# Limits for VectorE's exp tiles by segment, a new searched plan, and tie-breaking offsets in a self-scheduled Conformer block

One core of one Trainium2 chip. The metric is the device time in microseconds (us) of that core, as the median of repeated executions; the kernel before takes 931.73 us (three runs, 931.69 to 931.85). "The trace" is one profiled execution, with the start and length of every instruction on TensorE (PE; its weight loads are PEld), VectorE (DVE), ScalarE (ACT) and GpSimd (POOL).

## The reference

One Conformer block in bfloat16 on two sequences of 4000 tokens, width 144, 4 heads of 36. The softmax of the attention is the large part.

```python
B, T, D, K, H = 2, 4000, 144, 5, 4
x = x + 0.5 * (silu(layernorm(x) @ w_ff1a) @ w_ff1b)          # FF1
q, k, v = split(layernorm(x) @ w_qkv)                         # 4 heads of 36
p = softmax(einsum('bhqd,bhkd->bhqk', q, k) * 36 ** -0.5)     # 2 x 4 x 4000 x 4000
x = x + (p @ v) @ w_o
a, b = split(layernorm(x) @ w_pw1)
c = depthwise_conv5(a * sigmoid(b), dw)
x = x + silu(c) @ w_pw2
x = x + 0.5 * (silu(layernorm(x) @ w_ff2a) @ w_ff2b)          # FF2
return layernorm(x)
```

## The kernel before

The kernel works in 16 chunks of 500 tokens. A tile of the softmax is a block of keys times 500 queries for 4 heads; most tiles are 128x1000 in PSUM. Instructions are not written down in their final order. The kernel is a program of coroutines ("threads") with a list scheduler that runs while the kernel is built: it keeps an estimated clock for every engine, picks the thread that can go next, and records its instruction. The finished list is then replayed with semaphores. So the order on each engine is fixed when the chip runs it, and waits are as long as reality makes them.

```python
# Rec.op: what the planner thinks of an instruction
start = ready = self.free[eng]
for d, raw in o.deps:
    if d.eng != eng or d.q is not None or (raw and eng != "pe"):
        ready = max(ready, d.done + self.SEM[eng])
# ...
self.free[eng] = o.t1 = start + cost          # cost is a number that the kernel gives
```

The exp of a tile is done by one ScalarE instruction, or by VectorE in seven (per half a linear step that writes the bits of a 16-bit float, then a correction over both halves). `due()` decides on VectorE, from limits that are partly tables by segments of 21 tiles (`now("...")`) and partly constants (FDVE, FEQ; PRELAG in `lag()`).

```python
def emit_exp(n, lo, hi):                                           # ScalarE's way
    # ...
    op("act", "activation", PT[:, pt, :, :], PSV[:, lo:hi + 1, 0:CH], ACT.Exp, bias=0.0, scale=ATT_SCALE, ...)

def due():                                                         # VectorE's turn?
    n = n_s[0]
    if n >= NIT or not DVE_EXP or live_dve[0] >= now("LIVE") or early[0] >= now("EARLY") or lag():
        return False
    ph, c, t = its[n]
    if len(kv_done) < CPB and (len(kv_done) < FDVE or len(eq) < FEQ):    # the front: keys still missing
        return False
    return (t <= phases[ph][2] - 7 and c in q_done and keys_in(c, t + 6)
            and R.free["dve"] < R.free["pe"] + now("DSLACK") and R.free["pe"] > last_dve[0] + now("DGAP"))
```

The front is the time in which the keys and values of the first sequence are still being made (8 chunks); the tail is what is left after the last attention matmul. A layer norm is divided differently in these than in the middle, where all of it but the statistics is GpSimd's:

```python
def ln(c, bs, e=False):                                            # cut
    # bn_stats on VectorE
    calm = mode["front"] or mode["tail"]
    op("dve" if calm else "pool", "tensor_scalar", RS[..., 1, 0:n], ST[..., 2], 1.0 / D, LN_EPS, ...)
    op("pool", "tensor_tensor", RS[..., 0, 0:n], RS[..., 1, 0:n], NHALF, op=ALU.pow, ...)
    if not calm:
        op("pool", "tensor_scalar", RS[..., 2, 0:n], ST[..., 1], -1.0, None, op0=ALU.mult, ..., cost=0.3)
        for j in range(n):
            op("pool", "tensor_scalar", XN[..., j, :], X[...], RS[..., 2, j:j + 1], RS[..., 0, j:j + 1], ..., cost=XN_COST)
    elif mode["tail"] and R.free["act"] + XSLACK < R.free["dve"]:  # on ScalarE
        ...
    else:                                                          # on VectorE
        ...

# the tail: earliest thread first
S.run(min((q for q in c if q[1].req.eng == eng), key=lambda q: q[0] + (q[1].rank >= 0) * TFIRST)[1])
```

The softmax here doesn't subtract the row's maximum and nothing guards it: scores larger than these inputs give would overflow.

## Time and profile before

| stage | from the trace of before |
|---|---|
| first exp starts | 20.30 us |
| keys of the 8th chunk are copied, the front ends | near 121 to 122 us |
| first exp on VectorE | 89.05 us |
| last exp ends | 896.08 us |
| tail, from there to the last instruction's end | 33.47 us |
| exp tiles | 855 wide on ScalarE, 137 on VectorE |

All instructions go through one helper, line 169, so they are told apart by tiles: PT the exps, PS a PSUM bank, TH tanh, XN a normalized block, RS and ST the statistics of a norm, HT the FF products, WA and WB the FF weights. A matmul that writes PS from IDENT alone is a filler: its result is not used, and the scheduler puts it on TensorE where its clocks foresee a wait.

A reading used throughout: ScalarE's *work* between the first and last exp is the sum of counts times paces (0.884 us from the start of one wide exp to the next, 0.467 for a 500-wide tanh, and so on). The *loss* is the length of that stretch less the work. Before, that is 875.8 - 843.9 = 31.9 us.

### The profile page before, as it was taken

The numbers are of one execution on the slowest core, as the hardware profiler recorded it, in microseconds if no ns is written. First come the engines' busy times: TensorE is split into PE (matmuls) and PEld (weight loads), VectorE is DVE, ScalarE is ACT, GpSimd is POOL, SyncE is SP. The second block draws the span as 40 slices with busy tenths as digits, with TensorE's granted clock in tenths as the row PEclk, the third lists the DMA queues.
The fourth block names the chain that finished last, engine by engine and source line by source line (L and its number), as shares of the span: only waits on it lengthen the run. The fifth ranks groups of instructions, "written<-read, shape, count | busy, mean of one in ns | idle before, by whom it ended". The sixth has DMA issues, their size and how long they took to land.

```text
span 929.6 us, 26576 instructions
## 1 busy us (share of the span) xinstructions
PE 886.9 (95%) x11413; PEld 405.4 (44%) x11413; DVE 849.9 (91%) x1880; ACT 895.0 (96%) x1142; POOL 306.1 (33%) x520
## 2 busy tenths in 40 slices
PE   8999999999999999999999999999999999999997
PEld 7444433434344344344443443443444343434456
DVE  8886799999989999998999999898999999997997
ACT  6899999999999999999999999999999999999985
POOL 4220140182115412351512452225415331441433
PEclk9999999999999999999999999999999999999999
DMA  4000000000000000000000000000000000000000
GB/s 124 22 2 1 2 2 1 1 2 1 2 2 2 2 2 2 2 2 1 9 1 1 14 2 8 2 1 14 2 8 3 7 2 9 8 1 8 8 2 26
DMA packets 7449, 7.30 MB, mean 8 GB/s; under 512 B 2381, under 2 KB 7332, under 8 KB 7332
## 3 DMA queue, kind: packets, MB, share of 16 engines
q1 hardware_dynamic: 5918, 5.00, 1.8%
q8 instruction: 89, 1.46, 0.6%
q10 hardware_dynamic: 1414, 0.62, 0.3%
q14 instruction: 28, 0.23, 0.1%
HBM read 3.31 MB, written 2.30 MB: 6 GB/s over the span
## 4 chain that ended last, share of the span: by engine, by line
ACT 47%; PE 36%; DVE 14%; issue 1%; POOL 1%; DMA 0%; POOLq 0%; DVEq 0%
ACT PT L169 41%; PE PS L169 36%; DVE PT L169 8%; ACT TH L169 5%; DVE ST L169 2%; DVE HT L169 1%; DVE X L169 1%; DVE QT L169 1%; DVE OTF L169 1%; POOL RS L169 0%; DMA X<-in_x_dram 0%; DVE DG L169 0%; POOL XN L169 0%; DVE XN L169 0%; DVE XT L169 0%
## 5 line engine op out<-in xcount | busy, mean ns | idle before, releaser
L169 ACT ACTIVATE PT<-PS 128x1000 bf16<-128x1000 f32 (+1 forms) x871 | 802.4, 1053 | 6.8 <-PE PS L169 5.2
L169 PE MATMUL PS<-QT,KT 64*64 64x500 bf16 x3968 | 413.9, 385 | 20.3 <-ACT PT L169 14.2
L169 PE MATMUL PS<-PT,VA 64*37 64x500 bf16 x3968 | 353.4, 374 | 4.9 <-DVE OTF L169 2.2
L169 PEld LDWEIGHTS PS<-QT,KT 64*64 64x64 bf16 x3968 | 122.4, 104 | 219.7 <-ACT PT L169 139.1
L169 POOL TENSOR_SCALAR RS<-ST 125x4 f32<-125x4 f32 x112 | 41.6, 371 | 467.2 <-DVE ST L169 462.5
L169 DVE TENSOR_SCALAR PT<-PS 128x500 uint16<-128x500 f32 x274 | 183.0, 669 | 12.8 <-PE PS L169 11.5
L169 DVE TENSOR_TENSOR PT<-PT 128x1000 uint16<-128x1000 uint16 (+1 forms) x274 | 184.0, 676 | 1.5
L169 DVE TENSOR_SCALAR PT<-PT 128x1000 uint16<-128x1000 uint16 (+1 forms) x411 | 163.8, 415 | 2.3
L169 PEld LDWEIGHTS PS<-PT,VA 64*37 64x37 bf16 x3968 | 114.1, 95 | 111.1 <-issue 31.9
L169 POOL TENSOR_SCALAR XN<-X,RS 125x144 bf16<-125x144 bf16 x224 | 149.9, 680 | 5.8
L169 POOL TENSOR_TENSOR RS<-RS,NHALF 125x4 f32<-125x4 f32 (+1 forms) x103 | 100.5, 980 | 112.5 <-DVE RS L169 107.8
L169 ACT ACTIVATE TH<-PS 128x500 bf16<-128x500 f32 (+2 forms) x198 | 104.3, 549 | 5.0 <-PE PS L169 4.3
L169 DVE SCALAR_TENSOR_TENSOR HT<-TH,PS 128x500 bf16<-128x500 bf16 (+1 forms) x135 | 80.8, 614 | 9.6 <-ACT TH L169 9.4
L169 PE MATMUL PS<-XT,WA 72*128 72x500 bf16 (+2 forms) x288 | 73.8, 355 | 2.9 <-DVE HT L169 1.6
L169 DVE SCALAR_TENSOR_TENSOR X<-PS,X 125x288 bf16<-125x288 f32 x128 | 57.0, 451 | 15.3 <-PE PS L169 13.6
L169 DVE BATCH_NORM_STATS2 ST<-X 125x6 f32<-125x288 bf16 x160 | 65.5, 446 | 1.2 <-DMA X<-in_x_dram 1.0
L169 PE MATMUL PS<-WB,HT 128*125 128x144 bf16 (+1 forms) x640 | 52.8, 230 | 0.5 <-DVE HT L169 0.5
L169 PEld LDWEIGHTS PS<-WB,HT 128*125 128x125 bf16 (+1 forms) x640 | 44.1, 136 | 14.0 <-issue 4.2
L169 PE MATMUL PS<-IDENT,XN 125*72 125x125 bf16 x512 | 42.2, 221 | 2.5 <-DVE HT L169 1.3
L169 DVE COPY XT<-PS 72x1000 bf16<-72x1000 bf16 (+1 forms) x66 | 39.9, 609 | 3.1 <-PE PS L169 2.6
L169 PEld LDWEIGHTS PS<-IDENT,XN 125*72 125x72 bf16 x512 | 31.5, 112 | 21.0 <-issue 10.6
L169 PE MATMUL PS<-U,DG 128*128 128x250 bf16 (+5 forms) x204 | 34.3, 265 | 0.6 <-DVE PT L169 0.4
(88 smaller groups left out, 579.6 us busy)
## 6 DMA issues: line engine op xcount, KB each, us to landing
X<-in_x_dram SPq DMA_DIRECT2D x16, 140.6 KB
out_dram<-XN SPq DMA_DIRECT2D x13, 140.6 KB
out_dram<-XN SPq DMA_DIRECT2D x4, 70.3 KB
WA<-in_w_ff1a_dram ACTq DMA_DIRECT2D x1, 144.0 KB
WB<-in_w_ff1b_dram ACTq DMA_DIRECT2D x1, 144.0 KB, 2.6
WA<-in_w_ff2a_dram SPq DMA_DIRECT2D x1, 144.0 KB
WB<-in_w_ff2b_dram SPq DMA_DIRECT2D x1, 144.0 KB
WQKV<-in_w_qkv_dram ACTq DMA_DIRECT2D x1, 121.5 KB
```

What stands on the lines that cost most here:

```text
L169: ins = getattr(eng, o.name)(*o.a, **o.k)
```

## The change

Its intent: constants that limit VectorE's exps become tables, so that the search can set them by segment; the offsets FJ (front) and TJ (tail), looked up by a thread's number, let the search break ties between threads; two switches of the tail get other thresholds; and the matmuls of a chunk's conv remainder wait by rule for the copy of the edge. All tables were searched anew.

```diff
+    TJ = (0.0, 0, 0.0, 0.0, -0.3, ... 48 offsets, 12 of them not zero)
+    FJ = [0.0, ... 0.25, ... -0.25, ... 64 offsets, 2 of them not zero]
+    FLEX = 0.3
 ... (the tables AHEAD to BGPICK: all new values but nothing else)
         "DSLACK": (
-            0.4, 0.4, 0.4, 0.2, 0.2, 1.5, ...
+            0.4, 0.4, 0.4, 2.5, 1.5, 1.5, ...
+        "FEQ": (2, 2, 2, 1, 2, ... 49 entries),
+        "FDVE": (5, 5, 5, 5, 5, ...),
+        "PRELAG": (0.7, ...),
+        "LAGD": (1, 0, 1, 1, ...),
-    FDVE = 5
-    FEQ = 2
-    PRELAG = 0.7
-        if mode["tail"] and R.free["act"] < R.free["dve"]:
+        if mode["tail"] and R.free["act"] + FLEX < R.free["dve"]:
-    XSLACK = 0.5
+    XSLACK = 1.2
-            bk = yield need("pe", banks, dur=0.17)
+            bk = yield need("pe", banks, dur=0.17, cond=lambda: c in left_done)
-        if ... or lag():
+        if ... or now("LAGD") and lag():
-        if len(kv_done) < CPB and (len(kv_done) < FDVE or len(eq) < FEQ):
+        if len(kv_done) < CPB and (len(kv_done) < now("FDVE") or len(eq) < now("FEQ")):
 ... (three other sort keys take FJ of the thread's number; the conv rule has one more wait, for the last chunk)
-    S.run(min((...), key=lambda q: q[0] + (q[1].rank >= 0) * TFIRST)[1])
+    S.run(min((...), key=lambda q: q[0] + (q[1].rank >= 0) * TFIRST + TJ[q[1].no % len(TJ)])[1])
```

## The prediction

> **What bounds the kernel now.** I read the busy table and the slices of the page first, then the busy times by stretch, the groups by form, the merged timeline of ScalarE and TensorE, and last the counts of instructions per engine in the changed kernel's order. The kernel carries its own list scheduler: the tables in the diff steer which thread goes next, and the arithmetic is the same. So the question is where an engine has room, and whether the new order uses it.
>
> ```profile
> PE 886.9 (95%) x11413; PEld 405.4 (44%) x11413; DVE 849.9 (91%) x1880; ACT 895.0 (96%) x1142; POOL 306.1 (33%) x520
> ...
> DVE  8886799999989999998999999898999999997997
> ACT  6899999999999999999999999999999999999985
> ...
> ACT 47%; PE 36%; DVE 14%; issue 1%; POOL 1%; DMA 0%; POOLq 0%; DVEq 0%
> ```
>
> Three engines are above 90% and the chain of waits hops between them, but ScalarE is the fullest: it is at 9 in all slices but the first two and the last two. The busy times by stretch (columns: stretch, its length, then busy us and count of PE, PEld, DVE, ACT and POOL, clock, DMA share, GB/s) split this by stage:
>
> ```profile
> 20.30:44.30 24.00, 21.78 (x229) 11.61 (x228) 20.98 (x60) 19.85 (x34) 5.58 (x8) 1.00 0.10 36
> 44.30:67.00 22.70, 22.11 (x296) 9.52 (x294) 18.93 (x59) 22.38 (x29) 5.53 (x8) 1.00 0.01 3
> 67.00:93.00 26.00, 25.38 (x309) 10.78 (x308) 17.45 (x37) 24.64 (x33) 1.36 (x2) 1.00 0.00 1
> 93.00:896.00 803.00, 772.33 (x10017) 333.81 (x10016) 751.23 (x1577) 796.80 (x982) 272.25 (x458) 1.00 0.01 4
> 896.00:929.50 33.50, 26.89 (x333) 23.31 (x329) 25.54 (x90) 20.25 (x46) 10.80 (x19) 0.98 0.06 18
> ```
>
> From 93 to 896 us ScalarE is busy 796.8 of 803.0, or 99.2%: that stretch shortens only if ScalarE is given less, or starts closer together. From 44.3 to 93 (the rest of the front, in which keys and values are still being made) ScalarE is also nearly full, 47.0 of 48.7, but VectorE has 48.7 - 18.93 - 17.45 = 12.3 us idle. The tail, after the last exp, is 33.5 us in which ScalarE has slack; there TensorE is the fullest.
>
> ```profile
> L169 ACT ACTIVATE PT<-PS 128x1000 bf16<-128x1000 f32 x855 | 794.4, 1061 | 5.6 <-PE PS L169 4.0
> L169 DVE TENSOR_SCALAR PT<-PS 128x500 uint16<-128x500 f32 x274 | 183.0, 669 | 12.8 <-PE PS L169 11.5
> L169 DVE TENSOR_TENSOR PT<-PT 128x1000 uint16<-128x1000 uint16 (+1 forms) x274 | 184.0, 676 | 1.5
> L169 DVE TENSOR_SCALAR PT<-PT 128x1000 uint16<-128x1000 uint16 (+1 forms) x411 | 163.8, 415 | 2.3
> ...
> 453.52 15.24 ACT PT L169 x17
> ```
>
> The first row is the exp of one tile of scores on ScalarE; the next three are the VectorE substitute, two plus two plus three instructions a tile, 137 tiles. The last line is from the chain in order of time: 17 exps take 15.24 us, 0.896 each. (The row's 1.061 us contains the overlap of neighbours. The median from one start to the next is 0.884.) So one tile moved away frees 0.884 us of ScalarE and costs VectorE (183.0 + 184.0 + 163.8) / 137 = 3.87 us.
>
> **What the Trainium skill says.** "ScalarE: Activation LUTs", section "What ACT_TABLE_LOAD costs", gives one element per cycle at 1.2 GHz, which is 833 ns for 1000 elements, plus a fixed part, with neighbours overlapping. The 0.884 measured here is 51 ns above that, so the pace of the exp is nearly all elements, and no order of instructions makes one cheaper. "VectorE: DVE Perf Modes", section "The perf-mode tier table (the rule you actually need)", puts a 16-bit tensor_scalar in SBUF at 4x, tensor_tensor at 2x, and anything from PSUM at 2x at most. The trace agrees in rank: 415 ns, 676 ns and 669 ns, the last for half as many elements. The substitute costs VectorE over four times what it saves ScalarE and pays only where VectorE idles. "Perfetto Trace Analysis", section "Optimization Strategy", says that kernels can have several regimes and may gain by interleaving them; the 12.3 us of idle VectorE beside a full ScalarE is such a place.
>
> **The change, part by part.**
>
> *Front limits.* FDVE, FEQ, PRELAG and the lag test become tables by segments of 21 tiles. The front ends after some 84 tiles, so only the first four or five entries of FDVE and FEQ can act there; FDVE stays 5 in them and FEQ falls from 2 to 1 in segment 3 (tiles 63 to 83), where the slack for VectorE (DSLACK 0.2 to 2.5) is also opened and the gap (DGAP 4.0 to 3.5) cut. The switch on lag can do nothing in the front, since the lag test answers no before all keys are in. The counts in the order show the effect. VectorE has 280 half-tile exps instead of 274, so 140 tiles instead of 137; ScalarE has 852 exps instead of 855. All three come early: ahead of the key copies of the eighth chunk VectorE has done 5 tiles instead of 2. In the trace the first VectorE exp starts at 89.0 us and those copies at 121. Saving on ScalarE: 3 x 0.884 = 2.65 us. Cost on VectorE: 3 x 3.87 = 11.6 us, which fits the 12.3 us idle, if barely. TensorE's 4 + 4 matmuls a tile stay.
>
> *Other ScalarE work between first and last exp.* By counts it rises by one tanh of 128x500 and one copy, some 0.47 us each: +0.9 us. Net there: -1.7 us.
>
> *Front ties (FJ).* Two non-zero entries swap a few threads. ScalarE does 7 exps in both before the pause in them that lies at 28.4 to 44.3 us. In the pause it now does 18 instead of 14 wide tanh and one more narrow one, counted from the first exp: 4 x 0.467 + 0.258 = 2.1 us more. The exps resume later by about that, but the same tanh are missing afterwards. I count zero. The eighth chunk's keys now come after 75 score tiles instead of 84, so the front is over earlier, which moves work and removes none.
>
> *Middle.* All search tables are redone. Start-to-start paces times counts (855 x 0.884, 137 x 0.467, 29 x 0.154, 27 x 0.258, 16 half exps and 11 copies at 0.47) make 844 us of the 875 between the first and last exp's start, so 31 us are lost, 4 to 5 of them in the pause and the rest in crumbs. New tables may regain or lose a few of these. I take -0.3 us.
>
> *Tail (TJ, FLEX, XSLACK).* After the last attention matmul the new order leaves two 500-wide tiles of FF2's first layer (four matmuls) and four pairs of pw2 matmuls less on TensorE: 4 x 0.215 + 8 x 0.065 = 1.4 us by the paces of the tail. It also does one chunk of FF2 in 500-wide matmuls that was done in 250-wide halves; at 0.215 us for one and 0.1075 for the other that is the same time. So an estimate of the real work left there goes from 22.9 to 21.5 us. One layer norm goes back to GpSimd ahead of the tail: ScalarE normalizes 2 rows' sets instead of 8. Instead, one FF2 chunk goes through tanh, which gives VectorE five more products, 4 x 0.666 + 0.407 = 3.1 us. VectorE has 8 us idle in the tail, so half of that may show as waits.
>
> ```profile
> 921.03 2.04 PE L169 MATMUL PS<-WB,HT 128*125 128x144 bf16 x30
> 922.92 0.81 DVE L169 SCALAR_TENSOR_TENSOR X<-PS,X 125x288 bf16<-125x288 f32 x2
> 925.24 1.21 DVE L169 TENSOR_SCALAR XN<-X,ST,RS 126x144 bf16<-126x144 bf16 x4 [0.24 <-POOL RS L169]
> ```
>
> Here 30 closing matmuls come in one batch, three residuals, statistics and norms queue behind them, and the span ends 6.5 us after TensorE does. The new order ends with 10, the other 20 lying earlier: some 0.5 us less. Tail in sum: -1.9 us, of which I give 0.4 back for the waits: -1.5.
>
> *Last conv waits for edges.* A condition that orders emission, for one chunk, behind a GpSimd copy that is long done: 0.
>
> Sum: -2.65 + 0.9 - 0.3 - 1.5 = **-3.6 us**, 931.7 to about **928.1 us**.
>
> **Rivals.** (a) *The moved tiles return as waits.* VectorE also serves the front's tanh products and copies; with 11.6 us more in 12.3 of idle time, TensorE waits for banks and ScalarE for TensorE. For: ScalarE and TensorE are both at 97% there, and the front's waits of VectorE are for TensorE and ScalarE, not free choice. Then the 2.65 us are lost: about 931. (b) *The search found more than counts show.* For: 31 us are lost between exps, and nearly every table is new. Against: the old tables came from the same sort of search, and the gaps that the trace shows on ScalarE from 93 to 896 are only 6 us. It would give 924 to 925. (c) *The tail gets longer.* Tanh makes two engines do what Silu did in one, and TensorE fillers stay at 37 against 36, so the new order expects as much idle time. Then the tail gives +1 in place of -1.5: 930 to 931. (d) *The real times differ from the scheduler's table*, and the order loses where an engine comes late: perhaps +2 us on any of these.
>
> **Range and chances.** The core is -3.6; (a), (c) and (d) pull up by 2 to 3, (b) down by 3 to 4. The range is 924.5 to 931.0. Two per cent is 18.6 us; no stage has that to give (the whole tail is 33.5, the moved tiles 2.65), and the work is the same, so a slowdown of that size is as far. Faster by over 2%: 0.01. Within 2%: 0.98. Slower: 0.01.
>
> **What would show it.** Right: 852 wide exps on ScalarE; VectorE's busy time up by some 10 us, with the 44 to 93 us stretch near 90% where it was 75%; the last exp's end 1.5 to 2.5 us earlier than 896.1; the stretch after it about 32 us. Wrong: the last exp ends no earlier, with more idle time before ScalarE's exps or TensorE's score matmuls in the front (rival a); the last exp ends over 4 us earlier (b); the tail is 34 us or more (c).

## The result

The changed kernel takes 928.27 us (four runs, 928.17 to 928.39), the kernel before 931.71 us in the same rounds (931.69 to 931.85): 3.44 us less. The ratio is 0.9963, with a 95% interval of 0.9946 to 0.998; within 2%. The prediction was 928.1 us, and its direction, class and range held.

The page of the changed kernel, its busy times, two rows of the slices and the shares of the chain that ended last:

```profile
PE 886.4 (96%) x11406; PEld 400.7 (43%) x11406; DVE 861.9 (93%) x1900; ACT 888.8 (96%) x1133; POOL 307.9 (33%) x524
...
DVE  7998999999999998798999999999999999998987
ACT  5799999999999999999999999999999999999985
...
ACT 48%; PE 34%; DVE 14%; POOL 2%; issue 1%; DMA 0%; POOLq 0%; DVEq 0%
```

VectorE took on 861.9 - 849.9 = 12.0 us of work (some 9.3 of it for the three tiles: so much it sheds when they are given back below); ScalarE gave up 6.2 us in the whole execution. GpSimd's share of the chain, 1% before, is now 2%: a small sign of what the experiments come to in the end. The same stretches as in the prediction, with the ends of the last two moved to this kernel's (columns: stretch, its length, busy us and count of PE, PEld, DVE, ACT, POOL, then clock, DMA share, GB/s):

```profile
20.30:44.30 24.00, 22.89 (x208) 11.64 (x200) 22.50 (x60) 20.09 (x36) 4.90 (x8) 1.00 0.11 40
44.30:67.00 22.70, 22.24 (x352) 11.23 (x352) 20.68 (x65) 19.95 (x27) 6.45 (x9) 1.00 0.01 3
67.00:93.00 26.00, 24.95 (x328) 10.46 (x324) 21.69 (x47) 25.89 (x34) 2.11 (x3) 1.00 0.01 1
93.00:893.50 800.50, 773.88 (x9998) 331.02 (x9989) 756.05 (x1587) 794.52 (x980) 270.70 (x455) 1.00 0.01 4
893.50:926.40 32.90, 25.34 (x304) 21.29 (x302) 25.50 (x85) 17.24 (x37) 13.31 (x25) 0.94 0.08 23
```

From 44.3 to 93 us VectorE is now busy 20.68 + 21.69 = 42.4 of 48.7 us, or 87%; it was 75%. The stretch from 93 us to the last exp is 2.5 us shorter (800.5 against 803.0), and ScalarE is as full in it as before, 794.52 of 800.50, or 99.3%. That is what a bound that was relieved of work looks like: the same fullness, a shorter stretch.

The groups by form give the counts, and the merged timeline gives the first VectorE exp of the changed kernel (columns of the timeline: start, length, engine, line, operation, tiles, shapes):

```profile
L169 ACT ACTIVATE PT<-PS 128x1000 bf16<-128x1000 f32 x852 | 792.3, 1063 | 6.3 <-PE PS L169 5.1
```

```profile
65.90 0.68 DVE L169 TENSOR_SCALAR PT<-PS 128x500 uint16<-128x500 f32 x1 [0.93 <-PE PS L169]
```

Three exps moved, and VectorE's first exp comes at 65.90 us instead of 89.05. ScalarE's timeline at the last exp, before and then after:

```profile
893.70 2.38 ACT L169 ACTIVATE PT<-PS 128x1000 bf16<-128x1000 f32 x3
```

```profile
891.81 1.66 ACT L169 ACTIVATE PT<-PS 128x1000 bf16<-128x1000 f32 x2
```

The last exp ends at 893.70 + 2.38 = 896.08 before, and at about 893.46 after: 2.6 us earlier. Where the rest lies:

| part | before | after | difference |
|---|---|---|---|
| first exp starts | 20.30 | 20.58 | +0.28 |
| ScalarE's work to the last exp | 843.9 | 842.2 | -1.7 |
| ScalarE's loss there | 31.9 | 30.7 | -1.2 |
| tail | 33.47 | 33.05 | -0.42 |
| span of the trace | 929.6 | 926.5 | -3.0 |

The two profiled executions differ by 0.4 us less than the medians. The first row is only scatter: in the other traces of these two plans the first exp starts anywhere from 20.42 to 20.74 us.

The gain was not built up evenly. By the start of a score tile's exp (tiles counted from 0), the new order is 4.0 us *behind* at tile 20 (61.1 against 57.1 us), 0.8 ahead at tile 63, 3.1 ahead at tile 84 (119.4 against 122.4), 2.3 behind at tile 400 and 3.0 ahead at tile 990. A lead in the middle of such a plan says little; only where the last exp ends counts.

And the tail, of which I had expected -1.5 us, gave -0.4. The closing matmuls and the last normalization, after:

```profile
919.10 0.84 PE L169 MATMUL PS<-WB,HT 128*125 128x144 bf16 x10
```

```profile
921.74 1.21 DVE L169 TENSOR_SCALAR XN<-X,ST,RS 125x144 bf16<-125x144 bf16 x4 [0.15 <-POOL RS L169]
```

The closing batch has 10 matmuls instead of 30, as foreseen, but the time from TensorE's end to the end is 6.58 us where it was 6.48: the smaller batch bought nothing. TensorE itself ends 26.47 us after the last exp instead of 26.99.

### The profile page after: what moved, and what is told of

It is laid out like the page before. It is cut to its first block, busy times and chain, and to the rows that moved or that the text cites. A ratio compares the mean times of both kernels' runs of the same rounds, so it can differ in the third digit from the quotient of the medians.

```text
span 926.5 us, 26578 instructions
## 1 busy us (share of the span) xinstructions
PE 886.4 (96%) x11406; PEld 400.7 (43%) x11406; DVE 861.9 (93%) x1900; ACT 888.8 (96%) x1133; POOL 307.9 (33%) x524
## 4 chain that ended last, share of the span: by engine, by line
ACT 48%; PE 34%; DVE 14%; POOL 2%; issue 1%; DMA 0%; POOLq 0%; DVEq 0%
ACT PT L169 43%; PE PS L169 34%; DVE PT L169 7%; ACT TH L169 5%; POOL RS L169 1%; DVE ST L169 1%; DVE HT L169 1%; DVE X L169 1%; DVE QT L169 1%; POOL XN L169 1%; DVE XT L169 0%; DMA X<-in_x_dram 0%; DVE OTF L169 0%; DVE SW L169 0%; DVE XN L169 0%
## 5 line engine op out<-in xcount | busy, mean ns | idle before, releaser
L169 POOL TENSOR_SCALAR RS<-ST 125x4 f32<-125x4 f32 x114 | 51.2, 449 | 461.6 <-DVE ST L169 456.1
L169 DVE TENSOR_TENSOR PT<-PT 128x1000 f16<-128x1000 f16 (+1 forms) x280 | 188.4, 677 | 1.5
L169 DVE TENSOR_SCALAR PT<-PT 128x1000 uint16<-128x1000 uint16 (+1 forms) x420 | 170.3, 418 | 2.8
L169 POOL TENSOR_SCALAR XN<-X,RS 125x144 bf16<-125x144 bf16 x228 | 142.4, 636 | 5.9
L169 POOL TENSOR_TENSOR RS<-RS,NHALF 125x4 f32<-125x4 f32 (+2 forms) x101 | 98.5, 980 | 96.5 <-DVE RS L169 91.7
L169 ACT ACTIVATE TH<-PS 128x500 bf16<-128x500 f32 (+2 forms) x203 | 108.2, 560 | 5.7 <-PE PS L169 5.2
L169 DVE SCALAR_TENSOR_TENSOR X<-PS,X 125x288 bf16<-125x288 f32 (+1 forms) x128 | 57.2, 451 | 7.5 <-PE PS L169 6.6
L169 PE MATMUL PS<-IDENT,XN 125*72 125x125 bf16 (+1 forms) x512 | 42.4, 221 | 3.7 <-DVE XN L169 1.7
L169 PEld LDWEIGHTS PS<-IDENT,XN 125*72 125x72 bf16 (+1 forms) x512 | 31.2, 112 | 23.9 <-issue 12.6
L169 PE MATMUL PS<-U,DG 128*128 128x375 bf16 (+5 forms) x204 | 34.0, 265 | 0.0
```

Of the source, the lines that this page charges most:

```text
L169: ins = getattr(eng, o.name)(*o.a, **o.k)
```

## The experiments

Twelve kernels ran, on several chips. Except for the last call the kernel before ran at medians of 931.71 to 931.88 us in all of them, so I compare medians with 928.27 us directly. (In the first eight, one of seven runs of the kernel before took 941 us at a granted clock of 0.986, which pulls its mean up and the ratios down; the medians are free of this. One run each of five of the kernels, and two of another, took some 0.9 to 1.6 us longer than the rest of the same kernel, at a granted clock of 0.996 instead of 0.998 or more; the traces read below are all of the quicker kind.) One part needed no run: with the conv rule alone undone, the order of instructions on every engine is identical. Its effect is 0 by construction.

### Parts of the change undone

**The tail's rules.**

```diff
-    TJ = (48 offsets)    FLEX = 0.3    XSLACK = 1.2
+    TJ = (0.0,)          FLEX = 0.0    XSLACK = 0.5
```

> The changed kernel with TJ all zero, FLEX 0 and XSLACK 0.5. The order up to the tail is the same, so the last exp must end at 893.5 us again. Theory (the counts made the tail shorter, and a held-up GpSimd ate most of it; the tie table is worth little by itself): about 929.3, that is +0.5 to +1.5 on 928.3. Rival (the tail rules are what the gain is made of): 931 or more. Second rival (they do nothing): within 0.3 of 928.3.

Measured: 928.68 us (928.67 to 930.15; ratio 0.9956). The last exp ends at 893.45, as in the changed kernel, and the tail is 33.41 us instead of 33.05. The tail's rules are worth 0.4 us, between what the theory and the second rival gave them. The trace says more: without these rules the removed work is gone from the tail all the same. Fillers left out, TensorE is busy after the last exp for 25.05 us in the kernel before, 23.46 in the changed one and 23.00 in this one. So the other tables removed that work, which by itself gave almost nothing (33.47 to 33.41 us; the hold-up of GpSimd that is told of below stands in this run too), and nearly all that the tail gained came with its rules.

**The old plan with the new thresholds.** All tables and limits of before, no offsets; only FLEX and XSLACK are new.

> The plan of the kernel before (all its tables, 137 tiles on VectorE, no offsets) with only the two new tail limits, FLEX 0.3 and XSLACK 1.2. Theory (the gain sits ahead of the last exp): no gain, 931 to 933, last exp ending at 896.1 as before. Rival (the tail limits alone give the gain): 928 to 929.

Measured: 931.84 us (931.80 to 931.84; ratio 0.9985), tail 33.63 us. The thresholds do nothing for the old plan; the 0.4 us belongs to offsets that were searched for this one.

**The limits.** FDVE, FEQ, PRELAG and LAGD as the constants of before, all other tables new.

```diff
+        "FEQ": (2,) * 49, "FDVE": (5,) * 49, "PRELAG": (0.7,) * 49, "LAGD": (1,) * 49,
```

> The changed kernel with FDVE, FEQ, PRELAG and the lag test back to their constants. Its order has 134 tiles on VectorE and 858 wide exps on ScalarE, six more than the changed kernel. Theory (each exp on ScalarE is worth its pace of 0.884 us): 6 x 0.884 = 5.3 us later last exp, at 898 to 900 us, and 933 to 936 in all. Rival (the gain is a matter of order and waits, not of counts): last exp within 2 us of 893.5, time under 931.

Measured: 952.58 us (952.47 to 952.75; ratio 1.0207). A miss by far: I had expected a few us. ScalarE does 858 wide exps instead of 852, its work is 6.5 us more, its loss 10.7 us more, and the tail 7.1 us longer (40.11); these three make the 24.3 us. Up to 101 us the two kernels are nearly the same. It is what comes later that went wrong: the other tables were tuned to the exact course that the limits gave, by the number of the tile, and on another course they fit nothing. So this run does *not* say that the limits are worth 24 us. It says that a searched plan can't be taken apart by its parameters; the following runs change instructions and leave the plan alone.

It does settle one thing that the prediction had otherwise. With the limits of before, VectorE's first five tiles are the same as in the changed kernel: 25, 40, 49, 54 and 69 of the score tiles, the first at 65.8 us. Before, it has two that early, tiles 47 and 55. So the early tiles don't come from the new limits, whose first changed entry for the front, in segment 3, acts from tile 63 on only. They come with the other tables. In both new orders the fifth chunk's keys, for which the limit FDVE asks, are there at 62.5 us instead of 69.5; whether that is the reason was not tested.

**The front's offsets.** `FJ = [0.0]`.

> The changed kernel with the two non-zero front offsets (FJ) set to zero. ScalarE and GpSimd keep their order exactly, TensorE and VectorE swap a few instructions. Theory (I counted zero for the front ties): 928.0 to 928.6. Rival (the ties are what makes the front faster): 929 or more.

Measured: 928.35 us (928.12 to 928.55; ratio 0.9948). Nothing, as predicted.

### Which engine binds, with the plan held fixed

In each of these, instructions of known size are added without telling the scheduler (cost 0 on its clocks), so that everything else keeps its place.

**ScalarE.**

```diff
+    if stats["exp"] in (150, 200, ..., 700):                       # 12 places
+        op("act", "activation", SCR[:, 0:500], WB1..., ACT.Copy, cost=0.0)
```

> The changed kernel with 12 more ScalarE copies of 128x500 into scratch, one every 50 exps, the order otherwise unchanged: 12 x about 0.48 = 5.8 us more work on ScalarE. Theory (ScalarE sets the length from 93 us on): +5 to +6 us, about 934. Rival (three engines bind in turn): +2 to +3.

Measured: 933.74 us (933.39 to 934.98; ratio 1.0007). The copies hold ScalarE for 12 x 0.51 = 6.1 us; the last exp ends 5.45 us later: 0.89 of what was added. This is what the theory expected.

**VectorE.** The same with 14 additions of 128x736 in scratch, 14 x 0.449 = 6.3 us.

> The changed kernel with 14 more VectorE additions of 128x736 into scratch, one every 43 exps, the order otherwise unchanged: 14 x about 0.45 = 6.3 us more work on VectorE. Theory (ScalarE binds, VectorE has some slack in the middle): +1 to +2.5 us. Rival (VectorE binds as well): +5 to +6.

Measured: 932.89 us (932.25 to 933.50; ratio 0.9997), the last exp 3.95 us later: 0.63. A miss; I had expected at most 2.5. (Of the four runs two took 932.3 and two, at a clock of 0.996, 933.5; the trace is of the first kind.) With the order fixed, VectorE's queue has little slack, though ScalarE is at 99%. The additions have two inputs in SBUF, so by the lock told of below they may hold up GpSimd as well. Its busy time rose by 3.2 us, but TensorE waited for its XN no longer than before (1.4 us); I take the figure as VectorE's.

**TensorE.** The scores of 42 tiles are computed twice, 42 x 0.215 = 9.0 us.

> The changed kernel with the score matmuls of 42 tiles done twice (same result), 42 x 0.215 = 9.0 us more work on TensorE, the order otherwise unchanged. Theory (TensorE is close behind ScalarE): +2 to +5 us. Rival (TensorE binds): +8 to +9.

Measured: 932.01 us (931.79 to 933.51; ratio 0.9989), the last exp 3.46 us later: 0.38, in the expected range.

**VectorE in the front of the kernel before.** 26 such additions between its 9th and 60th exp, 26 x 0.452 = 11.75 us: what the prediction counted for the three tiles, in the room that it called idle.

> The kernel before with 26 VectorE additions of 128x736 into scratch between its 9th and 60th exp (46 to 101 us), 26 x about 0.45 = 11.7 us, as much as three exp tiles cost there, with nothing taken from ScalarE. Theory (that room was free): 0 to +1.5 us, up to 933.2. Rival a (VectorE's work returns as waits): +3 or more.

Measured: 935.93 us (935.84 to 935.98; ratio 1.0028) against 931.88, with the last exp 4.57 us later: 0.39. A miss: I had expected the idle room to swallow nearly all of it, and it is rival a's number that came. Idle time that the page shows is not room for any work. What comes unplanned stands before something that another engine waits for: from 44 to 106 us TensorE's waits for VectorE's copies and products rise from 1.0 to 3.8 us, and those of ScalarE's exps for TensorE from 0.5 to 2.8 us.

### The three tiles themselves

**Front tiles back to ScalarE.** In the changed kernel the first three VectorE tiles are computed by ScalarE, as two 128x500 exps each. The scheduler's clock of VectorE still counts the seven instructions that are left out, so TensorE's and GpSimd's orders are exactly those of the changed kernel.

```diff
 def dve_tile(n):
+    started[0] += 1
+    if started[0] in (1, 2, 3):
+        yield from act_tile(n)       # op("act", "activation", PT[:, z, hh, :], PSV[:, bk, 0:CH], ACT.Exp, cost=0.0)
+        return
```

> The changed kernel with its first three VectorE exp tiles (66 us on) computed by ScalarE, six exps of 128x500 in their place, while the plan still counts VectorE's time for them: TensorE and GpSimd keep their order exactly, the rest of VectorE and ScalarE too. ScalarE gets 6 x 0.47 = 2.8 us more, VectorE loses 3 x 3.35 = 10 us. Theory (the three tiles moved are the saving of the front): +2 to +2.8 us, 930.3 to 931.1. Rival (VectorE's load costs about as much as ScalarE is spared, as added VectorE work cost 0.4 to 0.6 of its length): -1.5 to +0.5.

Measured: 931.30 us (930.99 to 932.16, five runs; ratio 0.9996): 3.0 us more, just over the expected range, and nearly the kernel before. Its busy times by stretch in the front:

```profile
44.30:67.00 22.70, 21.83 (x344) 10.86 (x340) 20.10 (x64) 19.96 (x28) 6.45 (x9) 1.00 0.01 3
67.00:93.00 26.00, 24.10 (x304) 9.96 (x304) 13.08 (x28) 25.89 (x37) 1.36 (x2) 1.00 0.00 1
```

VectorE is relieved of 8.6 us in the second stretch (13.08 against 21.69), yet the execution is longer. The last exp ends at 896.35, 2.9 us later. That is the length of six half exps (6 x 0.47 = 2.8). The rival that the moved tiles return as waits would have left the time where it was. The figure is the tiles' worth in this plan: the six exps come unplanned, and a search without the three tiles might have placed them more cheaply.

**Middle tiles back to ScalarE.** The same for the 50th, 75th and 100th VectorE tile.

```diff
-    BACK = (1, 2, 3)
+    BACK = (50, 75, 100)
```

> The same for the 50th, 75th and 100th VectorE tile, in the middle. ScalarE gets 2.8 us more, VectorE loses 10 us. Theory (ScalarE binds by nine tenths, what VectorE sheds is worth less when the plan holds its place): +1.5 to +2.8. Rival (VectorE binds as well): -2 to +0.5.

Measured: 930.92 us (930.90 to 932.50, five runs; ratio 0.9995): +2.65 us, as expected, with the last exp at 896.30. So a tile on VectorE is worth the same in the middle, where VectorE is busy for 94% (756.05 of 800.50), as in the front. So idle time beside it is not needed for a placed tile to pay. That the front's idle time is what let the search place three more there is likely, but not shown.

### The tail's missing microsecond

The trace of the changed kernel shows a strange thing just before the tail. First GpSimd's timeline, then VectorE's in the same time:

```profile
888.22 4.24 POOL L169 TENSOR_SCALAR RS<-ST 125x4 f32<-125x4 f32 x1
892.57 1.79 POOL L169 TENSOR_SCALAR XN<-X,RS 125x144 bf16<-125x144 bf16 x4
...
896.17 1.79 POOL L169 TENSOR_SCALAR XN<-X,RS 125x144 bf16<-125x144 bf16 x4
```

```profile
888.03 0.67 DVE L169 TENSOR_TENSOR PT<-PT 128x1000 f16<-128x1000 f16 x1
...
890.46 1.26 DVE L169 TENSOR_TENSOR PT<-PT 128x1000 uint16<-128x1000 uint16 x2
891.63 0.74 DVE L169 TENSOR_SCALAR PT<-PT 128x1000 uint16<-128x1000 uint16 x2
892.29 0.67 DVE L169 SCALAR_TENSOR_TENSOR HT<-TH,PS 128x500 bf16<-128x500 bf16 x1
```

The negation of four means, 125x4 numbers, takes 4.24 us; the median of its group is 0.233. It is let go when VectorE passes from its exp instructions in SBUF to a product that reads PSUM. The Trainium skill, "SBUF — State Buffer", section "Who interferes with whom", says that VectorE and GpSimd share one pair of ports as an exclusive lock: VectorE takes it in its two-port modes, and with two SBUF inputs against a GpSimd instruction that reads SBUF, and the other engine is blocked for the whole instruction. The trace agrees: nine VectorE instructions of just these two kinds run end to end from 888.03 to 892.37, and the hold ends with them. It is no single case. Of the 114 instructions of this group, 60 overlap no VectorE instruction from PT to PT, and none of these takes over 0.29 us; 30 take over 0.4 us, and each of them ends within 0.1 us after the end of such an instruction. The scheduler, which charges 0.3 us for the negation, knows nothing of this. What it costs stands on TensorE:

```profile
898.01 0.63 PE L169 MATMUL PS<-IDENT,XN 125*72 125x125 bf16 x8 [1.06 <-POOL XN L169]
```

The theory: the 1.1 us that the tail owes is this hold-up.

**Late norms on VectorE.** Two norms before the tail use the tail's form.

```diff
-    calm = mode["front"] or mode["tail"]
+    calm = mode["front"] or mode["tail"] or n_s[0] >= NIT - 8
```

> The changed kernel with the layer norms that begin once all but 8 score tiles are issued taken to VectorE, as the tail does: the two norms that stand on GpSimd at 886.6 to 898 us, with its 4.24 us instruction, go. The order ahead of them is the same. Theory (GpSimd, held off by VectorE's run of exp instructions, delays the tail by about 1 us at 898.0): -0.5 to -1.5 us, about 927.3. Rival (the tail has other waits that take its place, or VectorE's added 2 us cost it): 0 to +1.

Measured: 931.49 us (931.36 to 931.57, five runs; ratio 0.9996), 3.2 us *more*: a miss. The hold-up is gone (the longest such instruction takes 2.38 us) and the transposes start at 896.29. But the edit let the scheduler make another tail, of 36.03 us, with other waits. ScalarE does six normalizations there instead of two, and TensorE waited for it, if only for 0.4 us at this place:

```profile
904.09 0.63 PE L169 MATMUL PS<-IDENT,XN 125*72 125x125 bf16 x8 [0.40 <-ACT XN L169]
```

Which of the new waits make the 3 us I did not trace further; but TensorE has 106 fillers in that tail instead of 37, so the plan itself foresaw most of them (a filler counts 0.056 us in it, so 3.9 us). It is the same mistake as with the limits: the edit changed the plan as well as the suspect.

**The two norms swapped, the plan kept.** Of the two norms, the one held up only leaves for the output, and the one behind it is what TensorE transposes. After planning is done, the first one's last five instructions and its store go behind the second. TensorE, VectorE and ScalarE keep their exact order, fillers included.

```diff
+    late = pool[492:497] + [its store]       # negation and four normalizations of the output's norm
+    R.ops[i:j + 1] = between + late           # behind pool[503], the last normalization of the other
     R.finish(group_qs=("w0", "w1", "w2", "w3"))
```

> The changed kernel with one edit after the plan is finished: on GpSimd, the norm that only leaves for the output (negation of its means and four normalizations, with its store) goes behind the norm whose result TensorE transposes at 898.01 us. The order of instructions on TensorE, VectorE and ScalarE is the same, fillers included. In the changed kernel the negation is held for 4.24 us while VectorE runs its exp instructions, and everything behind it on GpSimd is late; TensorE then waits 1.06 us. Theory (this hold-up is where about 1 us of the tail's missing gain went): the norm that TensorE waits for ends near 895.8 instead of 897.96, the wait of 1.06 us is gone or under 0.2, the stretch after the last exp falls from 33.05 to about 32.0 us and the time from 928.3 to about 927.2 us. Rival (other waits of the tail take its place, as in the run with the late norms on VectorE): the transposes start earlier but the tail stays within 0.3 us of 33.05 and the time within 0.4 us of 928.3. A tail over 33.5 us would fit neither.

Measured: 927.17 us (927.00 to 927.48, five runs; ratio 0.9913). GpSimd's timeline of this run, then TensorE's, then ScalarE's at the last exp:

```profile
887.89 4.54 POOL L169 TENSOR_SCALAR RS<-ST 125x4 f32<-125x4 f32 x1
...
893.93 1.79 POOL L169 TENSOR_SCALAR XN<-X,RS 125x144 bf16<-125x144 bf16 x4
```

```profile
896.79 0.60 PE L169 MATMUL PS<-IDENT,XN 125*72 125x125 bf16 x8
```

```profile
891.82 1.65 ACT L169 ACTIVATE PT<-PS 128x1000 bf16<-128x1000 f32 x2
```

The hold-up is no shorter than before, 4.54 us, and falls on the next norm's first instruction. But the norm that TensorE needs ends at 893.93 + 1.79 = 895.72 instead of 897.96, TensorE no longer waits for it, and the tail is 31.97 us: 1.08 less. The theory holds, and the rival that other waits take its place falls. On this last chip the kernel before ran at a median of 935.05 us (933.03 to 936.58), which I can't explain, so the ratio overstates the gain and should not be used. The reading rests on the trace: the last exp ends at 893.47, in the changed kernel at 893.46, so both ran alike up to there and only the tail differs. This version beats both kernels, by about 1.1 us and 4.5 us; the changed kernel did not run on this chip, so these compare medians across chips.

## Why the prediction was right, and which term was mis-sized

**ScalarE bounds the kernel.** Right, and now measured: a microsecond added costs 0.89 on ScalarE, 0.63 on VectorE, 0.38 on TensorE. But it isn't a clear bound with slack beside it. Unplanned VectorE work costs more than the prediction's picture of idle VectorE time allows. The prediction's cost of a tile on VectorE, 3.87 us, also adds up lengths that overlap: from start to start the seven take 2 x 0.589 + 2 x 0.590 + 3 x 0.329 = 3.35 us, so that a tile costs 3.8 times what it spares, not over four, and three tiles cost 10.0 us, not 11.6.

**Front limits, -2.65.** Right in size, for three tiles: giving them back costs 3.0 us, most of the whole gain. But the limits are not where they come from, as the run with the limits undone shows: it has the same first five VectorE tiles. The prediction read a cause out of the diff that the order doesn't have. Nor did the other reason given with it hold, that the substitute "pays only where VectorE idles": the middle tiles pay as much at 94%, and the idle room doesn't take unplanned work for free. My reading is that what decides is whether the plan has a place for the seven instructions, not the share of idle time.

**Other ScalarE work, +0.9.** Right: with the line above it makes -1.7, and the work by paces fell from 843.9 to 842.2.

**Front ties, 0.** Right: 928.35 without them. The exps do resume later after the pause, at 47.61 instead of 44.35 us, and this is made up by tile 63. But that isn't the ties' doing, as the prediction had it: without them ScalarE's order is the same to the last instruction.

**Middle, -0.3.** Too small: the loss fell by 1.2 us. Which tables did this can't be read from these runs, since undoing a part of them throws the plan off. It stays open.

**Tail, -1.5.** This is the mis-sized term: it measured -0.4. Its parts were -1.4 for TensorE's work, -0.5 for the closing batch and +0.4 for waits behind VectorE's five more products. With the two norms swapped, TensorE ends 25.40 us after the last exp, 1.6 less than the 26.99 of before, so the work was removed as counted, though by the other tables and not, as the prediction had it, by TJ, FLEX and XSLACK. The closing batch gave nothing (6.57 against 6.48 us). And the waits were 1.1 us more, not behind the products but behind GpSimd, held up by VectorE's exps. So the -1.5 is there once the hold-up is moved off the path (33.47 to 31.97).

**Conv rule, 0.** Right by construction.

**Rivals.** (a), tiles that return as waits, fell with the front tiles given back. (b), a larger find, fell: the loss shrank by 1.2, not by 4. (c), a longer tail, fell in sign. (d), real times other than the planner's, was real but half of the 2 us that I gave it: it is the hold-up.

**Of the signs named,** the counts, VectorE's 12.0 us and the 87% came as foreseen. The last exp came 2.6 us earlier, just outside the 1.5 to 2.5; the tail was 33.05 and not about 32. Two errors, 0.9 too little in the middle and 1.1 too much in the tail, nearly cancelled, so the close total is partly luck. The counts of the order carried the prediction; which parameter it gave them to was wrong in the front and in the tail.

## What to carry to other kernels

To find what a searched schedule gains from one of its parts, don't turn back the parameter: change the instructions and hold the plan fixed, or the new trajectory will drown the effect. And look in the run that turns it back for how far the order stays the same: what stands there before the first difference isn't owed to the parameter. When a tail or a handover gains less than its removed work, look for a small instruction with a very long time on an engine that nobody watches, and move what is urgent ahead of it. A planner needs to know which of its engines lock each other out.

## What the Trainium skill lacked or had wrong

- "SBUF — State Buffer", section "Who interferes with whom": it tells the lock by single instructions, "for the whole instruction". It lacks that a queue of VectorE instructions can keep it. Here a GpSimd instruction of 0.233 us (median) stood for 4.24 us, through nine VectorE instructions end to end, and for 4.54 us in the run with the norms swapped.
- "Perfetto Trace Analysis", section "Identifying the Most-Contended Engine": the engine with the highest occupancy is to be optimized first, where TensorE is not to be judged by its matmuls' busy time. That points to ScalarE here, and added work agrees (0.89 of its length). What it lacks is that the next engine may be little cheaper to load: work added to VectorE, at 93%, cost 0.63 of its length, and 11.75 us put into its idle time in the front of the kernel before cost 4.05 us.
- I found no page on how much a kernel's time differs from one chip to another: the kernel before had medians of 931.71 to 931.88 us in four sets of rounds and of 935.05 us on one other chip, at granted clocks of 0.995 to 0.998 there.
